# The first two chunk pairs of a Mamba-2 scan in chunks of 64 tokens instead of 128

## The chip, the cores and the metric

The kernel runs on one core of one Trainium2 chip. The metric is the device time of one execution in microseconds. The core has a matrix engine (TensorE, "PE" in the profile, with its weight loads as "PEld"), a vector engine ("DVE"), a scalar engine ("ACT"), a general engine ("POOL") and a queue engine that issues transfers ("SP"). Each executes its own instructions in the order in which the program lists them, and waits for the others by semaphores.

## What is computed

The reference is a Mamba-2 scan followed by a feed-forward block with a parametric ReLU, all in float32:

```python
# x (4, 8, 768, 32), a (4, 8, 768), B and C (4, 8, 768, 16); chunks of 32 tokens
la = log(clip(a, 1e-6, 1)); cum = cumsum(la within the chunk)
L  = exp(cum[i] - cum[j]) for i >= j, else 0
y  = ((C B^T) * L) @ x  +  (C @ state) * exp(cum)
state = exp(sum(la)) * state + sum_j exp(cum[-1] - cum[j]) * B[j] (outer) x[j]
# bridge: (batch, head, token, d) -> (batch * token, head * d) = (3072, 256)
h = X @ w_in                                  # w_in (256, 2048)
g = max(h, 0) + alpha * min(h, 0)
out = g @ w_out                               # w_out (2048, 256)
```

The size of the chunk is free: any size gives the same result, since the state carries over what lies before the chunk.

## The kernel before

**The scan.** The kernel works in chunks of `Q = 128` tokens, two at a time: a pair `gp` holds 256 tokens of one batch entry, and there are 12 pairs. For each pair it needs, per chunk and head, a matrix of decays between two tokens, the gram matrix C B^T, their product `dec` (times the input x gives the part within the chunk), the gain of the state `dps`, the state `new`, a copy of the state masked into head blocks (`sm`), and C decayed (`cd`, times `sm` gives the part from before the chunk). The results, turned into features by tokens, are copied into `xT`, which holds four chunks (a group of `GT = 512` tokens). Pairs 0 and 1, which fill the first group, are written out by hand in `first_two` (line 792); pairs 2 to 11 go through the generator `pair` (line 552) in stages that are woven into the feed-forward work. Pairs from 6 on (`half`) are already computed with each chunk in two halves of 64 tokens, in another way.

**The decays** come from a scan along the tokens on DVE: `dec[t] = a[t] * dec[t-1] + identity[t]`, started afresh by a zero in `a`. For pairs 0 and 1 the row of `a` of each head is spread to all partitions by matmuls with a column of the identity (`spread_rows`, line 490, for pair 0; `spread`, line 504, for pair 1), into PSUM; each of the eight scans then covers 512 columns (lines 908 and 855). Pairs from 2 on get the spread rows by a transfer from a scratch in DRAM (`z`) into the tile `abc`. The running product of decays from a chunk's start (`pf`, tile `ap`) and to its end (`pr`, turned into `prt`, which scales B into `bn` in `pair_loads`, line 465) are computed on 96 rows at a time: `rows_clamp`, `rows_scan`, `rows_out` (lines 411 to 441), and `rows_turn` (443) transposes `pr`, and with it the slopes `alpha`.

**The order of `first_two`.** There is no planner: the order of the text is the order on each engine's queue. Pair 0: spread, scans, transposes of B and C (`turned`, line 804: four PE transposes, one ACT copy `bc`, two ACT multiplies `cz`), gram, state gain (`added`, 827), products of gram and decays (`times`, 849; two of pair 0's four and one of pair 1's run on POOL, after an ACT copy of the gram into SBUF), then `outputs` (859), which multiplies by the masked state and by x and copies into `xT`. For pair 1 the order is: spread, transposes, then the first two hidden tiles of pair 0's tokens (`hidden_two`, line 1003), state gain, gram, the next two hidden tiles, outputs. Then the text outside goes on with hidden tiles of pair 1's tokens, with a pass of `hidden` (991) for every further tile of the group, one `output` (1028) a tile, four tiles behind, and pairs 2 to 4 in between.

`hidden_two` issues eight matmul instructions of 256 columns, two ACT multiplies by `s_alpha`, and returns the two DVE instructions (line 1023) that make the parametric ReLU:

```python
        for i in range(2):
            if t0 == 0:
                gts[g, f + i] = gp.tile([P, GT], F32, name="gt")
            nc.scalar.mul(gts[g, f + i][:, ts], hp[:, i * nt : (i + 1) * nt],
                          s_alpha[:, f + i : f + i + 1])
```

**The weights** arrive in 16 pieces as 64-bit numbers (`raw`) and are converted on the chip: `convert_a` (two or three ACT instructions, line 265 on, and one POOL instruction, 267), `sign` (DVE, 286), `convert_b` (DVE, 296), and `convert` (POOL, 318). `pieces[0]` and `pieces[1]` are the parts of `w_in` that the first four hidden tiles need. Piece 0 must be converted before the first `hidden_two`.

**Buffers.** PSUM has eight banks: two of the pool `ps_s` (`ss`), two of `ps_h` (`hp`, handed out by `spare`), and four single ones (`bank(0)` to `bank(3)`). The pool `gp` has 16 buffers for the hidden tiles `gt`. In the start all transfers but one (`rows`, by ACT) are issued by SP, in the order of the text: pair 0's loads, two weight pieces, `z` and `pf` to DRAM (`rows_out`), pair 1's loads, `pf` back for pair 1 (`load_second`), weight pieces, pair 2's loads.

After the first group, PE does the feed-forward block by a fast matrix product (`quad` and `product`, lines 1121 and 1089), which the change doesn't touch.

Of the kernel before, what the change touches and what calls it, by code (L numbers as in the profile page):

```python
# [9 lines left out]
F32 = mybir.dt.float32  # L10
# [12 lines left out]
def kernel(  # L23
# [196 lines left out]
    def load_second():  # L220

        rows = scratch["pf", 0].rearrange("(b h c) t -> b h (c t)", b=2, h=H)
        nc.sync.dma_start(out=loads["p", 1][3], in_=rows[0, :, 2 * Q : 4 * Q].unsqueeze(1)
                          .to_broadcast([H, N, 2 * Q]))
# [98 lines left out]
    def keep_warm(to, n, cols=2 * Q):  # L323

        for i in range(n):
# [6 lines left out]
    ident_h = const.tile([P, H * Q], F32, name="ident_h")  # L332
    nc.vector.tensor_copy(out=ident_h.rearrange("p (h t) -> p h t", h=H),
                          in_=ident.unsqueeze(1).to_broadcast([P, H, Q]))
# [17 lines left out]
    nc.vector.memset(ends[:, Q - 1 :], 1.0)  # L352

# [35 lines left out]
    def identity_bank():  # L389


        m5_bank.append(bank(3))
        nc.scalar.copy(out=m5_bank[0][:, HT:], in_=ident_h[:, :HT])
        ident_p.append(m5_bank[0][:, HT:])
# [15 lines left out]

    def rows_clamp(i):
        rows = loads.pop(("r", i))
        d0 = prep.tile([RW, SQ], F32, name="r0")
        nc.vector.tensor_scalar(out=d0[:, :Q], in0=rows, scalar1=1e-6, scalar2=1.0,
                                op0=ALU.max, op1=ALU.min)
        if i:
            nc.vector.tensor_scalar(out=d0[:, Q + 1 :], in0=rows[:, HQ + 1 :], scalar1=1e-6,
                                    scalar2=1.0, op0=ALU.max, op1=ALU.min)
        held[i] = d0
# [22 lines left out]

    def rows_turn(i, pr):

        ps = ss_tile() if i else ps_s.tile([P, 512], F32, name="ss")
        nc.tensor.transpose(ps[:, :RW], pr, ident[:RW, :RW])
        if i == 0:
            nc.tensor.transpose(ps[:, RW : RW + NF], al_n, ident[:NF, :NF])
        else:
            nc.tensor.transpose(ps[:, RW : 2 * RW], held["prs"], ident[:RW, :RW])  # L450
        t = bat.tile([P, RW], F32, name="prt")
        if i == 0:
            nc.scalar.copy(out=t, in_=ps[:, :RW])
        for v in range(2 if i else 0):
# [6 lines left out]
        if i == 0:  # L461
# [3 lines left out]
    def pair_loads(gp):  # L465
# [8 lines left out]
        else:  # L474
            pj = prt[i].rearrange("p (b h c) -> p b c h", b=2, h=H)[:, bi, c : c + 2]
# [6 lines left out]
    def first_a(ap, eng):  # L482

        z = prep.tile([P, 2, Q], F32, name="z", bufs=2)
        eng.memset(z[:, :, :1], 0.0)
        eng.tensor_scalar(out=z[:, :, 1:], in0=ap.rearrange("p (k t) -> p k t", k=2)[:, :, 1:],
                          scalar1=1e-6, scalar2=1.0, op0=ALU.max, op1=ALU.min)
        return z

    def spread_rows(z):  # L490

        ts = [bank(r) for r in range(4)]
        for k in range(2):
            for e in range(2):
                for r in range(4):
                    rs = slice(32 * r, 32 * r + 32)
                    row = 32 * r + N * e
                    cs = slice((2 * k + e) * Q, (2 * k + e + 1) * Q)
                    nc.tensor.matmul(ts[r][:, cs], ident[rs, row : row + 1].to_broadcast([32, P]),
                                     z[rs, k], start=(k == 0 and e == 0), stop=True,  # L500
                                     tile_position=(32 * r, 0), skip_group_check=True)
        return ts

    def spread(z, k, tile=lambda w: ss_tile()):

        ts = [tile(w) for w in range(2)]
        for q in range(4):
            for w in range(2):
                rs = slice(64 * w, 64 * w + 64)
                row = 64 * w + N * q  # L510
                nc.tensor.matmul(ts[w][:, q * Q : (q + 1) * Q],
                                 ident[rs, row : row + 1].to_broadcast([64, P]), z[rs, k],
                                 start=(q == 0), stop=True, tile_position=(64 * w, 0),
                                 skip_group_check=True)
        return ts
# [276 lines left out]
    def first_two():  # L792


        nat0, _, xt0, ap0 = loads["p", 0]

        dec = [work.tile([P, 2, H, Q], F32, name="dec") for i in range(2)]
        first = dec[0].rearrange("p a b t -> p (a b t)").rearrange(
            "p (r c) -> p r c", r=4)
        by_bank = first.rearrange("p r (k e t) -> p r k e t", k=2, e=2)  # L800
        pf0 = prep.tile([P, Q], F32, name="pf")
        new = {}
# [13 lines left out]

        def gram_of(bc, cz, banks):
            gram = [t.rearrange("p (k h t) -> p k h t", k=2, h=2) for t in banks]
            for k in range(2):
                for r in range(4):  # L820
                    rs = slice(32 * r, 32 * r + 32)
                    nc.tensor.matmul(gram[r][:, k].rearrange("p h t -> p (h t)"), bc[rs, k],
                                     cz[rs, :, k], start=True, stop=True,
                                     tile_position=(32 * r, 0), skip_group_check=True)
            return gram

        def added(dps, bn, xt):
            for k in range(2):
                for r in range(4):
                    rs = slice(32 * r, 32 * r + 32)  # L830
                    nc.tensor.matmul(dps[rs, k], bn[:, k, rs],
                                     xt[:, k, 2 * r * D : 2 * (r + 1) * D],
                                     start=True, stop=True, tile_position=(0, 32 * r),
                                     skip_group_check=True)

        def mask(sm, new, ks):
            n = ks.stop - ks.start
            nc.gpsimd.tensor_tensor(
                out=sm.rearrange("p k (g m) -> p k g m", g=2),
                in0=new[:, ks].unsqueeze(2).to_broadcast([P, n, 2, 2 * D]),  # L840
# [3 lines left out]
        def copied(gram):  # L844
            g0 = op.tile([P, GT], F32, name="o_sb").rearrange("p (k h t) -> p k h t", k=2, h=2)
            nc.scalar.copy(out=g0, in_=gram)
            return g0

        def times(i, r, gram, eng=nc.vector):
            o = dec[1][:, :, 2 * r : 2 * r + 2] if i else by_bank[:, r]  # L850
            eng.tensor_tensor(out=o, in0=gram, in1=o, op=ALU.mult)

        def decays(k, w, t):
            ws = slice(512 * w, 512 * w + 512)
            nc.vector.tensor_tensor_scan(out=dec[1][:, k].rearrange("p h t -> p (h t)")[:, ws],
                                         data0=t, data1=ident_h[:, ws], initial=0.0,
                                         op0=ALU.mult, op1=ALU.add)

        def outputs(i, tiles, st, cd, xt, ws, warm=0):
            y = [t[:, : 2 * Q].rearrange("p (k t) -> p k t", k=2) for t in tiles]  # L860
            keep_warm(y[ws[0]].rearrange("p k t -> p (k t)"), warm)
            begun = False
            for k in range(2):
                if st[k] is None:
                    continue
                for q in range(4):
                    qs = slice(32 * q, 32 * q + 32)
                    for w in range(KC):
                        hs = slice(64 * w, 64 * w + 64)
                        nc.tensor.matmul(y[w][qs, k], st[k][hs, qs], cd[hs, k],  # L870
# [601 lines left out]
```

## Time and profile before

| what | value |
|---|---|
| median of 3 runs | 358.48 us (358.33 to 358.49) |
| profiled execution, its own time | 358.82 us |
| span of the profiled execution | 357.1 us |
| granted TensorE clock | 1.000 |
| first hidden tiles' matmuls (line 1011) start | 18.02, 21.35, 25.01 us |
| first matmul of line 996 starts | 28.94 us |
| end of the scans of pair 0 (line 908) | 10.99 us |
| end of the last scan of pair 1 (line 855) | 20.07 us |

The span runs from the first to the last instruction of the execution, and times within it count from its start. The profile's page gives the busy time of each engine, the chain of waits (the work that ended last, followed back step by step), and the groups of instructions by line, with their count, busy time and the mean duration of one in ns. "x32 128x64" is 32 instructions on 128 partitions by 64 columns; a float32 matmul call appears as two instructions. A matmul's duration includes its way through the array, so that durations of neighbours overlap; the distance between two starts is what the engine spends on one.

### The profile page before, as it was taken

How to read it: one execution, taken by the hardware profiler on the slowest of the kernel's cores; microseconds unless marked ns; L12 is line 12 of the kernel's file. 1: busy time of each engine (PE TensorE's matmuls, PEld its weight loads, DVE VectorE, ACT ScalarE, POOL GpSimd, SP SyncE). 2: the span in 40 equal slices, each digit the busy share in tenths (PEclk: the TensorE clock that was granted, in tenths of full speed). 3: DMA queues.
4: the chain of work that ended last, by engine and by line, in shares of the span. 5: the costliest groups of instructions: out<-in, count | busy, mean ns of one | idle time of the engine just before them, and what ended most of it. 6: DMA issues, size and time to landing. Idle time of an engine off the chain costs nothing.

```text
span 357.1 us, 7561 instructions
## 1 busy us (share of the span) xinstructions
PE 350.5 (98%) x2894; PEld 289.0 (81%) x2894; DVE 240.0 (67%) x467; ACT 174.0 (49%) x387; POOL 205.0 (57%) x221
## 2 busy tenths in 40 slices
PE   8899999999999999999999999999999999999995
PEld 8676666578888888888888888888888888888884
DVE  6987986998748856857747856757856633653363
ACT  3577666535355346345345445345445344444431
POOL 4876668589938855725646626647527535533520
PEclk9999999999999999999999999999999999999999
DMA  7899999608255403403513423513001002002004
GB/s 112 175 189 299 334 202 255 143 16 168 89 97 125 98 2 75 104 2 75 96 39 74 91 48 68 93 49 64 10 4 29 0 2 31 0 0 32 0 1 91
DMA packets 105470, 30.19 MB, mean 85 GB/s; under 512 B 79881, under 2 KB 101337, under 8 KB 105433
## 3 DMA queue, kind: packets, MB, share of 16 engines
q1 hardware_dynamic: 105048, 29.52, 37.7%
q8 instruction: 23, 0.38, 0.4%
q10 hardware_dynamic: 384, 0.18, 0.2%
q14 instruction: 15, 0.11, 0.1%
HBM read 26.32 MB, written 3.37 MB: 83 GB/s over the span
## 4 chain that ended last, share of the span: by engine, by line
PE 93%; SPq 3%; DMA 1%; ACT 1%; issue 0%; DVE 0%
PE bank L1108 33%; PE hp L1133 29%; PE bank L1034 8%; PE hp L996 6%; PE ss L1133 6%; SPq L188 2%; PE hp L1011 2%; PE ss L758 1%; PE ss L702 1%; DMA nat<-in_C_dram 1%; PE bank L1101 1%; PE ss L750 1%; PE ss L776 1%; PE ss L713 1%; PE ss L589 1%; PE ss L768 0%
## 5 line engine op out<-in xcount | busy, mean ns | idle before, releaser
L1190 POOL TENSOR_TENSOR gt<-gt 128x512 f32<-128x512 f32 x58 | 74.1, 1278 | 21.1 <-DVE gt L1118 16.3
L1108 PE MATMUL bank<-gt,w_out 128*128 128x256 f32 x320 | 83.5, 381 | 0.0
L1108 PEld LDWEIGHTS bank<-gt,w_out 128*128 128x128 f32 x320 | 60.1, 190 | 9.2 <-issue 1.0
L1118 DVE SCALAR_TENSOR_TENSOR gt<-hp,s_mul,gt 128x256 f32<-128x256 f32 x96 | 42.0, 479 | 29.1 <-ACT gt L1116 26.8
L1180 POOL TENSOR_TENSOR gt<-gt 128x512 f32<-128x512 f32 x20 | 25.4, 1268 | 62.6 <-DVE gt L1118 57.2
L1116 ACT ACTIVATE gt<-hp,s_alpha 128x256 f32<-128x256 f32 x96 | 40.3, 471 | 34.6 <-PE hp L1133 31.5
L1108 PE MATMUL bank<-gt,ws 128*128 128x256 f32 x224 | 55.9, 379 | 0.0
L1108 PEld LDWEIGHTS bank<-gt,ws 128*128 128x128 f32 x224 | 42.3, 190 | 5.6
L1133 PE MATMUL hp<-xs,w_in 128*128 128x256 f32 x160 | 41.9, 384 | 0.0
L1133 PE MATMUL hp<-xs,ws 128*128 128x256 f32 x160 | 41.2, 380 | 0.0
L1159 DVE TENSOR_TENSOR hp<-hp,u 128x512 f32<-128x512 f32 x20 | 14.0, 699 | 35.8 <-ACT u L1157 35.8
L1133 PEld LDWEIGHTS hp<-xs,ws 128*128 128x128 f32 x160 | 30.3, 190 | 4.3 <-POOL xs L1075 0.2
L1133 PEld LDWEIGHTS hp<-xs,w_in 128*128 128x128 f32 x160 | 29.7, 190 | 4.5
L1034 PE MATMUL bank<-w_out,gt 128*128 128x256 f32 x128 | 31.0, 384 | 0.0
L1034 PEld LDWEIGHTS bank<-w_out,gt 128*128 128x128 f32 x128 | 23.6, 190 | 6.5 <-issue 2.9
L1133 PE MATMUL ss<-xT,w_in 128*128 128x256 f32 x96 | 24.6, 379 | 0.0
L996 PE MATMUL hp<-xT,w_in 128*128 128x512 f32 x48 | 22.7, 596 | 0.2 <-DVE gt L1023 0.2
L616 POOL TENSOR_TENSOR sm<-state,bmask 128x256 f32<-128x256 f32 (+1 forms) x10 | 6.2, 619 | 28.9 <-DVE state L613 28.9
L532 DVE TENSOR_TENSOR_SCAN dec<-abc,bank 128x192 f32<-128x192 f32 x48 | 22.7, 522 | 0.0
L1148 ACT COPY m<-hp 128x512 f32<-128x512 f32 x8 | 4.7, 586 | 35.7 <-PE hp L1133 35.7
L1157 ACT COPY u<-hp 128x512 f32<-128x512 f32 x20 | 11.7, 585 | 19.4 <-PE hp L1133 19.4
L1118 DVE SCALAR_TENSOR_TENSOR gt<-c,s_mul,gt 128x256 f32<-128x256 f32 x40 | 20.6, 555 | 0.0
(204 smaller groups left out, 618.3 us busy)
## 6 DMA issues: line engine op xcount, KB each, us to landing
abc<-z SPq DMA_DIRECT2D x24, 192.0 KB
raw<-in_moe_w_in_dram SPq DMA_DIRECT2D x8, 512.0 KB
raw<-in_moe_w_out_dram SPq DMA_DIRECT2D x8, 512.0 KB
abc<-z SPq DMA_DIRECT2D x8, 512.0 KB
out_dram<-o_sb SPq DMA_DIRECT2D x32, 64.0 KB
nat<-in_B_dram SPq DMA_DIRECT2D x26, 64.0 KB
nat<-in_C_dram SPq DMA_DIRECT2D x24, 64.0 KB
xt<-in_x_dram SPq DMA_DIRECT2D x12, 128.0 KB
```

Of the source, the lines that this page charges most:

```text
L188: nc.sync.dma_start(out=nat[:, i, k].rearrange("p (h n) -> p h n", h=H), in_=src[b, :, ts, :].rearrange("h p n -> p h n"))
L532: nc.vector.tensor_tensor_scan(out=dv[:, o : o + SQ], data0=abc[k][:, s : s + SQ], data1=ident_p[0][:, :SQ], initial=0.0, op0=ALU.mult, op ...
L996: nc.tensor.matmul(hp, w_in[:, k, f * P : (f + 1) * P], xts[g][:, k], start=(k == 0), stop=(k == KC - 1))
L1034: nc.tensor.matmul(pos[0][t // 2][:, t % 2], gt[:, t * Q : (t + 1) * Q], w_out[:, f], start=(f == 0 and t % 2 == 0), stop=(f == NF - 1), s ...
L1108: nc.tensor.matmul(ms[g][i][:, h], w, blocks[g, z][n][:, p], start=(q == 0 and h == 0), stop=(q == NQ - 1), skip_group_check=True)
L1116: nc.scalar.mul(o[:, p], h[:, p], s_alpha[:, fs[p]])
L1118: nc.vector.scalar_tensor_tensor(out=o[:, p], in0=h[:, p], scalar=s_mul[:, fs[p]], in1=o[:, p], op0=ALU.mult, op1=ALU.max)
L1133: nc.tensor.matmul(to[:, p], w(2 * z + p), b, start=start and p == 0, stop=True, skip_group_check=True)
L1157: nc.scalar.copy(out=u2, in_=A)
L1159: nc.vector.tensor_tensor(out=Y, in0=Y, in1=u2, op=ALU.add)
L1180: nc.gpsimd.tensor_tensor(out=tc_, in0=g22, in1=g12, op=ALU.subtract)
L1190: eng.tensor_tensor(out=o, in0=x0, in1=x1, op=ALU.subtract)
```

## The change

Pairs 0 and 1 are computed in chunks of 64 tokens. A pair then has four chunks `c`, of which two lie on the lower half of the partitions and two on the upper half (`k, j = divmod(c, 2)`: `k` is the old chunk of 128, `j` the half of it). A matrix of decays is 64 by 64 instead of 128 by 128: a scan covers 256 columns instead of 512, and so does a product with the gram, whose four products per pair all run on DVE from PSUM. Spread, gram, state gain and products with x are issued for each half by itself, with 64 instead of 128 rows or columns of the array. There are four states a pair instead of two, with as many masked copies. B, C and x are loaded as before and lie as before in SBUF.

Since pairs from 2 on keep chunks of 128, the rows of decays are made twice: once for chunks of 64 (`rows_short`, for pairs 0 and 1, written to a DRAM scratch `short`), and once as before (`rows_clamp`, now on POOL for the first half of the rows, `rows_scan`, `rows_out`), later in the order. Constants and small tiles for this are put into four buffers of `gp` (`lent`) and one of `xsp`. The order of `first_two` is changed with it; in pair 1 the transposes now come after the first hidden tiles.

The core of the diff:

```diff
     def load_second():
-        rows = scratch["pf", 0].rearrange("(b h c) t -> b h (c t)", b=2, h=H)
+        rows = scratch["short", 0].rearrange("(b h c) t -> b h (c t)", b=2, h=H)
...
-    ident_h = const.tile([P, H * Q], F32, name="ident_h")
-    nc.vector.tensor_copy(out=ident_h..., in_=ident.unsqueeze(1).to_broadcast([P, H, Q]))
+    ident_q = const.tile([P, 4 * HQ], F32, name="ident_q")
+    for v in range(2):
+        vs = slice(HQ * v, HQ * (v + 1))
+        nc.vector.tensor_copy(out=ident_q[vs].rearrange("p (c t) -> p c t", c=4),
+                              in_=ident[vs, vs].unsqueeze(1).to_broadcast([HQ, 4, HQ]))
...
+    lent = [gp.tile([P, 4, Q], F32, name="gt", tag="gt") for i in range(4)]
+    ends_q = lent[3][:, 0]
+    nc.vector.memset(ends_q, 0.0)
+    nc.vector.memset(ends_q[:, HQ - 1 :: HQ], 1.0)
+    starts_r = lent[3][:, 1]
+    nc.gpsimd.memset(starts_r, 0.0)
+    starts_a = lent[0][:, :2].rearrange("p k t -> p (k t)")
+    nc.gpsimd.memset(starts_a, 0.0)
...
+    def rows_short(r, rows):
+        clamp(nc.vector, starts_r[:RW, ::HQ], rows[:, ::HQ])
+        nc.vector.memset(r[:, ::HQ], 0.0)
+        pr = lent[3][:RW, 2]
+        nc.vector.tensor_tensor_scan(out=pr[:, ::-1], data0=r[:, 1:][:, ::-1],
+                                     data1=ends_q[:RW, ::-1], initial=0.0, ...)
+        rpf = lent[3][:RW, 3]
+        nc.vector.tensor_tensor_scan(out=rpf, data0=r[:, :Q], data1=starts_r[:RW], ...)
+        scratch["short", 0] = dr.tile([RW, Q], F32, name="short0")
+        held["short"] = rpf
+        return pr
...
+        def spread(z):
+            ts = [bank(r) for r in range(4)]
+            for e in range(2):
+                for r in range(4):
+                    rs = slice(32 * r, 32 * r + 32)
+                    row = 32 * r + N * e
+                    for j, hs in enumerate(halves):
+                        o = ts[r][hs, : 2 * Q].rearrange("p (k e t) -> p k e t", k=2, e=2)
+                        nc.tensor.matmul(o[:, :, e], ident[rs, row : row + 1]
+                                         .to_broadcast([32, HQ]), z[rs, :, hs], start=e == 0,
+                                         stop=True, tile_position=(32 * r, HQ * j), ...)
+            return ts
+        def scan(i, r, t):
+            nc.vector.tensor_tensor_scan(out=dec[i][:, r], data0=t[:, : 2 * Q], data1=ident_q, ...)
         def gram_of(bc, cz, banks):
...
-                    nc.tensor.matmul(gram[r][:, k].rearrange("p h t -> p (h t)"), bc[rs, k],
-                                     cz[rs, :, k], start=True, stop=True,
-                                     tile_position=(32 * r, 0), skip_group_check=True)
+                    for j, hs in enumerate(halves):
+                        o = banks[r][hs, (2 + k) * Q : (3 + k) * Q]
+                        nc.tensor.matmul(o.rearrange("p (e t) -> p e t", e=2), bc[rs, k, hs],
+                                         cz[rs, :, k, hs], start=True, stop=True,
+                                         tile_position=(32 * r, HQ * j), skip_group_check=True)
+        def x_products(y, xt, i):
+            for w in range(KC):
                 for k in range(2):
                     for q in range(4):
                         h = 4 * w + q
+                        for j, hs in enumerate(halves):
+                            d = dec[i][hs, h // 2].rearrange("p (k e t) -> p k e t", k=2, e=2)
+                            nc.tensor.matmul(y[w][j][32 * q : 32 * q + 32, k],
+                                             xt[hs, k, h * D : (h + 1) * D], d[:, k, h % 2],
+                                             tile_position=(HQ * j, 32 * q), ...)
+        def state_products(y, i, cd):
+            for c in range(4):
+                k, j = divmod(c, 2)
+                if i or c:
+                    s = sm[i][:, c - 1] if c else sm[0][:, 3]
+                    for w, ws in enumerate(halves):
+                        nc.tensor.matmul(y[w][j][:, k], s[ws], cd[ws, k, halves[j]], ...,
+                                         tile_position=(HQ * w, 0), skip_group_check=True)
+        def copy_out(i, y):
+            for w in range(KC):
+                o = xts[0][:, w, 2 * i * Q : 2 * (i + 1) * Q].rearrange(
+                    "p (k j t) -> p j k t", k=2, j=2)
+                for j in range(2):
+                    nc.scalar.copy(out=o[:, j], in_=y[w][j])
...
+        z0 = first_a(ap0, nc.vector, lent[1][:, :2])
+        sp = spread(z0)
+        prq = rows_short(rq, rows)
+        clamp(nc.vector, starts_a[:, ::HQ], ap0[:, ::HQ])
+        nc.sync.dma_start(out=scratch["short", 0], in_=held.pop("short"))
+        load_pair(1)
+        load_second()
+        rows_clamp(0)
+        for r in range(4):
+            scan(0, r, sp[r])
+        nc.vector.tensor_tensor_scan(out=pf0, data0=z0..., data1=starts_a, ...)
+        rows_turn("short", prq)
+        tp = spare()
+        bc0, cz0 = turned(nat0, tp)
+        bn0 = pair_loads(0)
+        cd0 = decayed_c(bc0, pf0)
+        z1 = first_a(loads["a", 1], nc.gpsimd, lent[1][:, 2:])
         pr = rows_scan(0)
         rows_out(0)
-        load_pair(1)
-        load_second()
         load_next(2)
         load_pair(2, False)
...
         hp = spare()
         keep_warm(hp, 6, Q)
+        gram_of(bc0, cz0, sp)
+        dps = dps_in([hp, tp])
+        added(dps, bn0, xt0)
+        for r in (0, 1):
+            times(0, r, sp[r])
+        states(0, dps, pf0)
+        for r in (2, 3):
+            times(0, r, sp[r])
+        mask(0, slice(0, 3))
+        slopes(alpha)
         convert_a(*pieces[0])
+        y = places([hp, tp], [ss(), ss()])
+        sp = spread(z1)
         xts[0] = xtp.tile([P, KC, GT], F32, name="xT")
+        x_products(y, xt0, 0)
+        state_products(y, 0, cd0)
+        copy_out(0, y)
+        sign(*pieces[0])
+        for r in (0, 1):
+            scan(1, r, sp[r])
+        convert_b(*pieces[0])
+        for r in (2, 3):
+            scan(1, r, sp[r])
+        convert_next()
         convert_a(*pieces[1])
+        rows_turn(0, pr)
+        bn1 = pair_loads(1)
         sign(*pieces[1])
         convert_next(first=False)
+        prelus = [hidden_two(0, 0, 0, spare())]
+        own = [ss(), ss()]
+        bc1, cz1 = turned(nat1, own[1])
+        cd1 = decayed_c(bc1, pf1)
+        mask(0, slice(3, 4))
+        dps = dps_in(own)
+        added(dps, bn1, xt1)
+        states(1, dps, pf1)
+        gram_of(bc1, cz1, sp)
+        mask(1, slice(0, 4))
+        for r in range(4):
+            times(1, r, sp[r])
         slope_signs()
         convert_a(*pieces[2])
         prelus.append(hidden_two(0, 2, 0, spare()))
         prelus[0]()
         convert_next(first=False)
         prelus[1]()
+        y = places(own, [bank(0), bank(1)])
+        x_products(y, xt1, 1)
+        state_products(y, 1, cd1)
+        copy_out(1, y)
...
     load_next(2)
-    rows_clamp(0)
     FIRST = 4
     first_two()
```

## The prediction

> **What bounds the kernel now.** I read the page's busy shares first, then its chain of waits, then busy time by stage, then the timeline of the first 30 us. The first windows below are the start, the last three all that follows (columns after the width: busy us of PE, PE's weight loads, DVE, ACT, POOL, then clock and DMA share).
>
> ```profile
> PE 350.5 (98%) x2894; PEld 289.0 (81%) x2894; DVE 240.0 (67%) x467; ACT 174.0 (49%) x387; POOL 205.0 (57%) x221
> ...
> PE 93%; SPq 3%; DMA 1%; ACT 1%; issue 0%; DVE 0%
> ```
>
> ```profile
> 9.00:18.00 9.00, 7.50 (x120) 5.40 (x121) 8.90 (x11) 5.15 (x12) 8.14 (x11) 1.00 0.86 175
> ...
> 24.95:28.90 3.95, 3.72 (x16) 2.87 (x16) 3.38 (x7) 2.96 (x8) 1.95 (x2) 1.00 1.15 174
> 28.90:60.00 31.10, 31.06 (x202) 19.77 (x203) 25.10 (x42) 21.32 (x42) 21.50 (x23) 1.00 1.04 292
> ```
>
> The reader is to see two regimes. From 28.9 us on PE has 0.04 us of idle in 31.1, and none from 60 to 350; a matmul's busy time overlaps its neighbour's, but the chain agrees (each L996 group starts when the L1034 group before it has issued). So what moves the first matmul of L996, at 28.94, moves the end by as much. Before 25 us PE waits, and from 9 to 18 us DVE is busy 8.90 of 9. The change lies wholly in that start. These lines set its pace:
>
> ```profile
> 14.35 2.33 DVE L855 TENSOR_TENSOR_SCAN dec<-bank,ident_h 128x512 f32<-128x512 f32 x2
> 16.34 1.26 POOL L318 TENSOR_TENSOR w_in<-wr,wg 128x512 uint32<-128x512 uint32 x1
> 17.29 0.58 ACT L810 COPY bc<-hp 128x512 f32<-128x512 f32 x1 [0.61 <-PE hp L807]
> 17.90 0.91 ACT L813 ACTIVATE cz<-bc,par 128x256 f32<-128x256 f32 x2
> 18.02 1.97 PE L1011 MATMUL hp<-xT,w_in 128*128 128x256 f32 x8 [0.77 <-ACT bc L810]
> 20.08 0.84 ACT L1017 ACTIVATE gt<-hp,s_alpha 128x256 f32<-128x256 f32 x2 [1.27 <-PE hp L1011]
> 21.35 1.99 PE L1011 MATMUL hp<-xT,w_in 128*128 128x256 f32 x8
> 25.01 3.72 PE L1011 MATMUL hp<-xT,w_in 128*128 128x256 f32 x16
> 28.94 1.96 PE L996 MATMUL hp<-xT,w_in 128*128 128x512 f32 x4 [0.21 <-DVE gt L1023]
> ```
>
> The four L1011 groups are the milestones: 18.02 (after the w_in piece at 17.60 and pair 1's transposed B and C, late by DMA, at 17.87), 21.35, 25.01, and L996 at 28.94. Pair 1's gram products start at 20.27, with no wait: cz was ready at 18.81.
>
> **What the Trainium skill says.** "TensorEngine Tiling (Array Packing)", Key Properties: changing the tiling mode drains the array. The trace agrees: 16 gram issues of 53 ns are 0.85 us, but the next group starts 1.08 us later. "TensorE: Matmul & The Clock Gate", "Wait — 56ns, not 53.3ns?": matmuls never start closer than about 25 ns. The trace disagrees for column tiles: L758 issues 64 of 64 rows by 32 columns in 0.85 us, 13 ns each. I take the trace; the page prices a rival. "SBUF — State Buffer", "SBUF: two separate sides": DVE and POOL share a port pair held for a whole instruction. The trace agrees: L286, beside POOL's L318, took 1.30 us at 16.59, and 0.42 at 12.27.
>
> **Prices.** Scan of 256 columns: L538, four in 2.41 us, 0.60; of 512: 1.20. DVE product of 256: 0.42 (L1211). ACT copy of 128x128: 0.28, between 0.22 (64 columns) and 0.37 (256). POOL on 384 columns: 1.0, between 0.73 and 1.28. PE issue, from L499, L702 and L758: 53, 26 and 13 ns for 128, 64 and 32 output columns, two instructions per call, and 0.27 us to the last one's end.
>
> **Part 1, to the first hidden matmul: earlier by 1.6.** The first spread starts behind the warm matmuls, 4.6 either way. 32 x 26 ns + 0.27 end at 5.7, not 6.39. Four scans of 0.60 run to 8.15, pf0 (256 columns now) to 8.75, rows_scan and rows_out, moved here (0.42 + 0.40 + memsets), to 9.65. Gram cannot profit: it waits for nat0's four loads, transposes 0.57, bc 0.58, cz 0.91. The transposes started at 6.72 with no DMA wait shown, so the loads landed between about 6.0 (two microseconds from the last issue's start at 3.85 are my estimate, from rows: issued 0.79, used by 3.36) and 6.72; I take 6.6, gram at 8.95, bank 0 complete at 9.75. DVE: two products to 10.64; added(0), the ACT copy of state 0 to 10.82; three states of 0.28 to 11.7; two products to 12.55, where before it was 12.35 for all that. The new spread reuses all four banks, so it stalls at its fourth until 12.55; bank 0 is complete at 13.05. sign hides in that. Two scans to 14.25, L296 0.69 to 14.95, POOL's L318 1.26 to 16.25, first L1011 at **16.4** instead of 18.02. POOL is in time: mask to 12.5, the slopes moved behind it (0.69), L267 to 13.8. xT is ready at 16.0: 64 products 1.0 from 13.15, 12 state products of 128 columns 0.75, four copies.
>
> **Part 2, to pair 1's gram: 0.6 later.** The hidden group now stands ahead of pair 1's transposes on PE, and on ACT its two multiplies (0.84) stand ahead of bc and cz. ACT takes them only when the eight matmuls have ended (20.08 after 19.99 in the trace). So: hidden to 18.4; transposes issued at 18.3, done by 18.95; multiplies to 19.3; bc to 19.88; added(1), in the same bank as bc's source, 19.9 to 20.5; cz to 20.8; gram at **20.85** against 20.27. PE is idle for about 1.3 us of this, with gram1 and the second hidden group queued behind, and DVE's four products behind gram1. The 1.6 gained is gone: 0.55 by the transposes that no longer lie in a wait, the rest by ACT's 0.84 and the 1.49 of bc and cz, formerly beside the hidden group.
>
> **Part 3, to the third L1011 group: 1.25 later.** Gram 1.05 to 21.9, hidden 1.92 to 23.82. DVE's states and four products end at 23.45, beside it. Then 64 products 1.0 (before 32 at K=128 with the copy of the first half beside the second), 16 state products 0.95 (before 0.60 for 32), now last: 25.77. The bank of y00 is complete at 25.62, of y01 at 25.83, two copies follow: **26.25** against 25.01. The added 0.65 over part 2 is PE 0.2 and copies that nothing covers.
>
> **Part 4, to L996: 1.15 later.** PE would be there at 26.25 + 3.72 = 29.97. On ACT: the last two copies to 26.77, convert_a 0.68 + 1.14 to 28.6, multiplies to 29.44, second L1023 to 29.95, the handover of 0.15: **30.1** against 28.94. The wait that cost 0.21 is still there.
>
> **Costed at nothing.** ident_q for ident_h (DVE, 0.77 of copy less two small ones) and new memsets: behind the warm matmuls to 4.58; uncovered, 0.3. POOL's two memsets and rows_clamp (about 1 us): POOL idles 3.3 us to 7.14. The gram copies and POOL products that go (ACT 1.8, POOL 4.3) free engines that wait elsewhere; what is late next is the scans' conversion, counted. Lent tiles take 4 of 16 gt buffers: the sixteenth hidden tile comes tens of us later. SP: short (48 KB, one issue of 0.4) takes the place of z and pf ahead of pair 1's loads, so nat1 comes 0.4 us sooner, needed 1.4 later; z and pf move behind load_second, and pair 2's ap<-pf, queued directly behind two weight loads, may now make SP wait for pf to land, up to 2 us, with pair 2's B, C, x and weight loads behind it. The cover: SP was blocked anyway in the x load issued at 19.79 (4.40 us for what takes 0.6). Without it, pair 2's scans (36.75, loads issued 27.3) have some 3 us to spare. Unseen; bounds -0.2 to +0.5, taken 0.
>
> **Sum.** +1.15 on the profiled execution's 358.82 (span 357.1, 1.7 around it) is 359.97; its own time lies 0.34 above the median shown, so 358.48 + 1.15 = **359.6**.
>
> **Rivals.** (a) *Not slower*: ACT's wait in part 2 does not appear. If cz is ready when added(1) has issued, at 19.5 instead of 20.8, gram starts 1.35 sooner and the sum is -0.2: 358.3, and a DVE that keeps its floor in part 1 (0.5 sooner if nat0 lands at 6.0, gram no longer the gate) makes it 357.8. For it: ACT is the least busy engine, 49%. Against: the program order on ACT and the end-of-bank wait at 20.08. Deciding point: gram1 before 19.6. (b) *Heavier*: small tiles pay the page's 25 ns. Each 64-product block grows by 0.75, pair 1's wholly on the path, pair 0's by 0.35 beyond the w_in piece: +2.25, 360.7. Against it L758's 13 ns; for it, that L758 mixes 64 and 128 columns, and no group of 64 alone is in the trace. (c) The halves don't free DVE (scans on 256 columns as slow as 0.9 in such company): +1.8 in part 1, about 361.4; L538 speaks against, I fold it into (b).
>
> **How the numbers follow.** About 0.2%, 0.72 us, is what a measurement of this kernel can tell from no change. My steps 0.52 (358.9 to 360.4; 0.06 of it under 0.72), rival (a) 0.28 (0.12 below -0.72), (b) with (c) 0.20. Slower 0.46 + 0.20 = 0.66, same 0.06 + 0.16 = 0.22, faster 0.12. The range 358.0 to 360.9 leaves out about 0.12 below and 0.08 above.
>
> **What would show it.** Right: first L1011 group near 16.4, gram1 waiting for ACT's cz at about 20.8, third group near 26.2 after two short copies, DVE idle before states(1), PE dense after 30. Wrong: gram1 before 19.6, or L758-like issues at 25 ns, or any new wait on PE after 30 us, which I hold impossible from the profile except pair 2's late loads.

## The result and the profile after

| | before | after |
|---|---|---|
| median (lowest to highest) of 4 runs | 358.40 us (358.22 to 358.49) | 360.93 us (360.74 to 361.46) |
| profiled execution, its own time | 358.82 us | 360.92 us |
| its span | 357.1 us | 359.2 us |
| its granted TensorE clock | 1.000 | 0.986 |

The change makes the kernel slower: the ratio is 1.0067, with a 95% interval of 1.0054 to 1.008. That is +2.53 us, where +1.15 was forecast; 360.93 lies 0.03 above the upper end of the range. The two profiled executions differ by 2.10 only, because what follows the start of PE's last group takes about 0.4 us longer in before's (4.5 us to the end of the span, against 4.0). The last group on PE starts at 352.63 before and at 355.16 after, and this difference is again 2.53.

One condition is needed to read the numbers below: executions of one kernel differ in the granted clock of their first 20 us, so runs whose mean clock is 0.998 or more are called *full clock*, the others *dropped*, and medians are given for each.

The page of the kernel after: busy times, the TensorE clock in 40 slices of 9 us, and the chain's shares by engine.

```profile
PE 351.0 (98%) x2999; PEld 289.5 (81%) x2999; DVE 238.1 (66%) x481; ACT 172.5 (48%) x389; POOL 203.8 (57%) x221
...
PEclk9679999999999999999999999999999999999999
...
PE 93%; ACT 1%; issue 1%; POOL 1%; DVE 1%; SPq 1%; DMA 1%; POOLq 0%
```

The busy shares and the chain hardly moved. The second line is what is new: slices two and three, 9 to 27 us, have 6 and 7 tenths of the clock where before had all of it. In steps of a quarter of a microsecond the clock falls to one half at 11.52 and is back at 21.76 us. The busy time by stage (width; busy us of PE, weight loads, DVE, ACT, POOL with instruction counts; clock; DMA share; GB/s) is therefore shown in stretches of 3.41 us that end at 11.52, a third of the 10.24 between the two; why, comes with the experiments. Kernel after:

```profile
4.69:8.11 3.42, 3.18 (x50) 2.40 (x48) 3.23 (x7) 1.49 (x5) 1.01 (x2) 1.00 1.11 163
8.11:11.52 3.41, 1.69 (x73) 1.02 (x72) 3.17 (x12) 1.70 (x4) 2.43 (x4) 1.00 0.96 302
11.52:14.93 3.41, 3.19 (x92) 2.58 (x94) 2.98 (x7) 0.04 (x1) 2.13 (x6) 0.50 0.82 97
14.93:18.35 3.42, 3.07 (x17) 2.53 (x16) 1.85 (x4) 2.12 (x7) 2.13 (x3) 0.50 0.72 144
18.35:21.76 3.41, 3.12 (x11) 2.08 (x9) 0.31 (x1) 1.38 (x3) 2.02 (x2) 0.50 0.94 295
21.76:25.17 3.41, 2.88 (x70) 2.18 (x70) 2.61 (x9) 2.03 (x4) 2.47 (x4) 1.00 1.02 150
```

PE is busy for 1.69 of the 3.41 us ahead of the drop; it is idle from the end of the state gain at 9.63 to 11.74 but for eight spread matmuls (kernel after; L862 is the state gain, L833 the spread of pair 1, which waits first for POOL and then for DVE's products):

```profile
9.10 0.53 PE L862 MATMUL hp<-xt,bn 64*32 64x64 f32 x32
10.61 0.45 PE L833 MATMUL bank<-gt,ident 32*64 32x128 f32 x8 [0.99 <-POOL gt L425]
11.74 1.45 PE L833 MATMUL bank<-gt,ident 32*64 32x128 f32 x24 [0.68 <-DVE dec L854]
```

At half clock a busy microsecond does about half the work: eight hidden matmuls take 3.67 us instead of 1.97 (below). The kernel before, in the stretch ahead of the drop and during it:

```profile
8.11:11.52 3.41, 2.70 (x47) 2.00 (x47) 3.41 (x5) 2.10 (x5) 2.70 (x7) 1.00 1.00 313
11.52:21.76 10.24, 9.25 (x127) 6.72 (x125) 9.29 (x14) 5.89 (x12) 9.22 (x11) 1.00 0.88 176
```

In this stretch PE also ran two matmuls of ones in the kernel before, which the change leaves out:

```profile
13.30 1.14 PE L326 MATMUL ss<-const-float32-1.0 128*128 128x256 f32 x4
```

DVE is indeed freed by the change: 5.14 us in those 10.24, formerly 9.29, and 6.71 in the run e9 below, where the clock stays at 1.00. From 31.42 on PE is as dense as it was: 28.54 us of the 28.58 to 60 are busy.

The timeline of the kernel after (start, duration, engine, line, operation, count; in brackets the idle time before it and what ended it), in the lines that answer to the milestones of before; L1043 is the old L1011, L1028 the old L996, L849 pair 1's gram:

```profile
14.84 1.27 POOL L318 TENSOR_TENSOR w_in<-wr,wg 128x512 uint32<-128x512 uint32 x1 [1.03 <-DVE wr L296]
16.60 3.67 PE L1043 MATMUL hp<-xT,w_in 128*128 128x256 f32 x8
20.06 1.06 PE L815 MATMUL ss<-ident,nat 128*128 128x128 f32 x4
20.37 0.84 ACT L1049 ACTIVATE gt<-hp,s_alpha 128x256 f32<-128x256 f32 x2 [2.45 <-POOL w_in L318]
21.16 0.59 ACT L818 COPY bc<-ss 128x512 f32<-128x512 f32 x1
21.78 0.91 ACT L821 ACTIVATE cz<-bc,par 128x256 f32<-128x256 f32 x2
22.74 0.70 PE L849 MATMUL bank<-cz,bc 32*64 32x128 f32 x32 [0.49 <-ACT cz L821]
23.37 1.99 PE L1043 MATMUL hp<-xT,w_in 128*128 128x256 f32 x8
27.54 3.72 PE L1043 MATMUL hp<-xT,w_in 128*128 128x256 f32 x16 [0.35 <-ACT xT L917]
31.46 1.96 PE L1028 MATMUL hp<-xT,w_in 128*128 128x512 f32 x4 [0.21 <-DVE gt L1055]
```

The first hidden group starts 1.42 us sooner than before, but its eight matmuls take 3.67 us instead of 1.97, and the transposes behind it take 1.06 (0.60 at full clock, in e9 below). Pair 1's gram waits for ACT's cz, as forecast, and the third hidden group and L1028 start 2.5 us later than before.

### The profile page after: what moved, and what is told of

Read it like the earlier page. It is cut to its first block, busy times and chain, and to the rows that moved or that the text cites. A ratio compares the mean times of both kernels' runs of the same rounds, so it can differ in the third digit from the quotient of the medians.

```text
span 359.2 us, 7798 instructions
## 1 busy us (share of the span) xinstructions
PE 351.0 (98%) x2999; PEld 289.5 (81%) x2999; DVE 238.1 (66%) x481; ACT 172.5 (48%) x389; POOL 203.8 (57%) x221
## 3 DMA queue, kind: packets, MB, share of 16 engines
HBM read 26.32 MB, written 3.42 MB: 83 GB/s over the span
## 4 chain that ended last, share of the span: by engine, by line
PE 93%; ACT 1%; issue 1%; POOL 1%; DVE 1%; SPq 1%; DMA 1%; POOLq 0%
PE bank L1140 33%; PE hp L1165 28%; PE bank L1066 8%; PE hp L1028 6%; PE ss L1165 6%; PE ss L762 1%; PE ss L706 1%; PE hp L1043 1%; PE bank L1133 1%; PE ss L754 1%; PE ss L780 1%; PE ss L717 1%; DMA nat<-in_C_dram 1%; POOL w_in L318 1%; PE ss L593 1%
## 5 line engine op out<-in xcount | busy, mean ns | idle before, releaser
L1028 PE MATMUL hp<-xT,w_in 128*128 128x512 f32 x48 | 22.7, 596 | 0.2 <-DVE gt L1055 0.2
```

The costliest lines, as they stand in the source:

```text
L1028: nc.tensor.matmul(hp, w_in[:, k, f * P : (f + 1) * P], xts[g][:, k], start=(k == 0), stop=(k == KC - 1))
```

## The experiments

Four theories stood against each other. **Clock**: the change leaves PE idle after pair 0's state gain, and it leaves out the `2` in `outputs(…, (1, 0), 2)`, two matmuls of ones whose result nothing uses, which ran at 13.30 before; the clock falls. **Small tiles**: the issues of 64 by 32 themselves cost more or pull the clock down. **Order**: pair 1's gram waits for ACT, because hidden tiles stand ahead of the transposes; moving these gains what the chunks of 64 were to give. **Weights** ("theory 4" where an expectation counts them): time that is won in the start is lost again at 36 to 49 us, where the weight pieces arrive.

Medians in us, with the number of runs; e1 to e4, e5 to e8, and e9 to e11 each ran on one chip, with the kernel before.

| run | overall | ratio to before [95%] | full clock | dropped | before, full clock |
|---|---|---|---|---|---|
| e1_warm | 359.78 | 1.0027 [1.0012, 1.0043] | 359.23 (12) | 361.05 (10) | 358.91 (39) |
| e2_order | 359.75 | 1.0024 [1.0012, 1.0036] | none | 359.75 (6) | 358.91 |
| e3_warm_order | 359.33 | 1.001 [1.0, 1.002] | 359.02 (9) | 359.58 (5) | 358.91 |
| e4_before_cold | 359.30 | 1.0017 [1.0002, 1.0032] | 358.74 (2) | 359.37 (9) | 358.91 |
| e5_after_again | 361.35 | 1.0059 [1.004, 1.0079] | none | 361.36 (8) | 359.00 (55) |
| e6_full_warm | 359.65 | 1.0023 [1.0007, 1.0039] | 359.58 (17) | 361.70 (5) | 359.00 |
| e7_full_warm_split | 359.79 | 1.0029 [1.0012, 1.0046] | 359.53 (15) | 361.61 (7) | 359.00 |
| e8_best | 358.89 | 0.999 [0.9975, 1.0005] | 358.83 (18) | 360.21 (3) | 359.00 |
| e9_full_warm3 | 359.10 | 1.0019 [1.0004, 1.0035] | 359.08 (20) | 361.88 (2) | 358.82 (36) |
| e10_order_split2 | 358.93 | 0.9994 [0.9982, 1.0005] | 358.82 (12) | 359.30 (2) | 358.82 |
| e11_order_split2_raw4 | 358.53 | 0.9999 [0.9978, 1.0019] | 358.31 (10) | 360.93 (4) | 358.82 |

### Keeping PE busy: e1, e5, e6, e9

e1 adds eight matmuls of ones (128 columns) in the idle stretch:

```diff
         added(dps, bn0, xt0)
+        others = [ss(), ss()]
+        keep_warm(others[0], 8, Q)
```

> The changed kernel with eight idle matmuls of 128 columns after pair 0's state gain, where PE waits from 9.5 to 11.7 us. Theory 1 (the clock): the changed kernel left out the two warm matmuls that stood before pair 0's outputs, PE idles most of 9.5 to 11.7, and the granted clock falls to 0.5 until about 20.6; with PE kept busy the clock stays at 1.0, the first hidden group starts near 16.2 and takes 1.95 instead of 3.67, pair 1's gram starts near 20.8 instead of 22.74, line 1028's first matmul near 30.0 instead of 31.46, and the time is 359.3 to 359.8. Rival (small tiles): matmuls on quarter arrays don't count as activity, so the clock falls all the same and the time stays within 0.3 of the changed kernel's 360.9. Rival (order alone): the clock falls but costs nothing, since ACT's order decides pair 1's gram; clock 1.0, time unchanged.

The changed kernel as it is dropped its clock in all twelve runs (four of the result, eight of e5); with the eight matmuls 12 of 22 runs keep it, at 359.23. The profile of e1 was one of the dropped ones (kernel e1, by stage):

```profile
9.72:13.14 3.42, 3.42 (x89) 2.93 (x78) 3.13 (x11) 1.47 (x3) 2.68 (x6) 1.00 1.06 264
13.14:16.55 3.41, 2.28 (x78) 1.72 (x79) 3.41 (x6) 1.14 (x5) 2.17 (x4) 1.00 0.88 113
16.55:19.96 3.41, 3.41 (x9) 2.55 (x10) 0.78 (x2) 0.94 (x3) 2.97 (x3) 0.50 0.65 156
19.96:23.38 3.42, 2.14 (x70) 1.48 (x69) 1.08 (x5) 3.17 (x7) 1.14 (x2) 1.00 1.05 289
```

The first hole is filled (3.42 of 3.42), the clock stays at 1.00 through it and through the small tiles behind it, and it falls at 16.55, after the next hole. It is back 3.41 us later; the first hidden group lies in that stretch and again takes 3.67 us.

e5 is the changed kernel again, unaltered.

> The changed kernel once more, on the chip of the next three, since the runs there scatter more than the first ones. Theory 1 (the clock falls after PE's idle from 9.5 to 11.7): the time is again some 2.5 above before, 360.5 to 361.2, with a clock of 0.5 for some 9 us. Rival (the clock's phase against the program decides each time): the time scatters over 2 us or more from run to run.

It gave 361.35, so the result holds on another chip. e6 fills the two later holes as well:

```diff
         for r in (0, 1):
             scan(1, r, sp[r])
+        keep_warm(sp[0][:, 2 * Q :], 6, Q)
...
         bc1, cz1 = turned(nat1, own[1])
+        keep_warm(sp[1][:, 2 * Q :], 4, Q)
```

> The changed kernel with idle matmuls in all three of PE's waits (8 after pair 0's state gain, 6 after its outputs, 4 behind pair 1's transposes, of 128 columns). Theory 1: the clock is 1.0 throughout, the first hidden group starts near 16.4 and takes 1.95, gram of pair 1 near 20.8, line 1028 near 30.0, which is the timetable of the prediction; time 359.2 to 359.8, 1.2 to 1.7 below the changed kernel on the same chip. Rival (ACT's order alone makes the loss): time within 0.4 of the changed kernel's.

17 of 22 runs keep the clock. But six are too many: they start at 16.04 and push the first hidden group to 17.56, 1.52 us behind their own start. e9 has three in their place, and 0.86 us from their start to the hidden group.

> As the kernel with idle matmuls in all three waits, but only three instead of six behind pair 0's outputs, where six ran past the arrival of the first weight piece and held the first hidden group back by a microsecond. Theory 1: at full clock the group starts at 16.4 to 16.7, pair 1's gram near 20.8 to 21.1, the third group near 25.6, line 1028's first matmul near 29.5 to 29.8, so that the changed kernel at full clock is 0.3 to 0.8 above before; runs in which the clock falls are some 1.8 longer. Rival: at full clock it is still over 1 above before, as the prediction's sum of 1.15 said.

20 of 22 runs keep the clock, at 359.08. Its profile (clock 0.999) shows the changed kernel's timetable without the drop, with fifteen matmuls of ones in its holes (e9's timeline; L1047 and L1032 are L1043 and L1028, L296 is DVE's part of the conversion of the first weight piece):

```profile
14.13 0.69 DVE L296 SCALAR_TENSOR_TENSOR wr<-wt,wr 128x512 uint32<-128x512 uint32 x1 [0.24 <-POOL wt L267]
16.31 1.98 PE L1047 MATMUL hp<-xT,w_in 128*128 128x256 f32 x8
20.69 0.70 PE L849 MATMUL bank<-cz,bc 32*64 32x128 f32 x32 [0.49 <-ACT cz L821]
25.49 3.72 PE L1047 MATMUL hp<-xT,w_in 128*128 128x256 f32 x16 [0.35 <-ACT xT L917]
29.41 1.96 PE L1032 MATMUL hp<-xT,w_in 128*128 128x512 f32 x4 [0.20 <-DVE gt L1059]
```

So the measured 2.52 at the last line (31.46 against 28.94) is 0.47 of timetable (29.41 against 28.94) and 2.05 of clock (31.46 against 29.41). This split compares single profiles. The medians agree on the second part: full clock against dropped within one kernel is 1.82 in e1, 2.12 in e6, 2.08 in e7 and, with only two dropped runs, 2.79 in e9. On the first, full clock against before at full clock gives +0.26 (e9), +0.32 (e1) and +0.58 (e6).

### Are small tiles to blame? e4

e4 takes the idle matmuls after the start out of the kernel *before*, most of whose tiles there have 128 rows or columns:

```diff
         hp = spare()
-        keep_warm(hp, 6, Q)
...
-        outputs(0, (ss(), ss()), (None, sm0[0][:, 0]), cd0, xt0, (1, 0), 2)
+        outputs(0, (ss(), ss()), (None, sm0[0][:, 0]), cd0, xt0, (1, 0))
```

> The kernel before without its idle matmuls after the start (six of 128 columns before pair 0's gram, two of 256 before its outputs). Theory 1: the clock falls here too, in chunks of 128, some 3 to 4 us after PE's waits at 8 to 11 us, and the time grows by 1 to 2.5, to 359.5 to 361. Rival (small tiles): without quarter arrays the clock stays at 1.0 and the time at 358.4 or a little below.

The clock drops in 9 of 11 runs, and the time goes up by 0.46 among those (359.37 against 358.91), less than the 1 to 2.5 expected. Its profile by stage:

```profile
5.50:8.91 3.41, 1.85 (x30) 1.18 (x22) 2.84 (x4) 1.66 (x5) 1.28 (x3) 1.00 1.05 171
8.91:12.33 3.42, 3.22 (x38) 2.25 (x40) 2.87 (x4) 1.21 (x4) 2.05 (x6) 0.50 1.08 317
12.33:15.74 3.41, 3.41 (x46) 3.10 (x44) 3.03 (x5) 2.47 (x5) 3.25 (x4) 0.50 0.60 55
15.74:19.15 3.41, 2.64 (x56) 1.98 (x41) 3.32 (x4) 2.24 (x5) 2.88 (x4) 1.00 1.02 186
```

An idle PE lowers the clock with large tiles too, and e9 runs all the small tiles at 1.00. Small tiles are neither needed for the drop nor enough for it. The drop costs a quarter of what it costs in the changed kernel: it is over at 15.74, and the first hidden group starts at 18.36 instead of 18.02. What a drop costs depends on what runs in it, and not on its length alone: e1's, half as long but with the first hidden group inside, costs 1.82.

**The length of a drop.** It is 10.24 us in the result's profile, 3.41 in e1's, and 6.83 in those of e2 (13.40 to 20.23), e4 (8.91 to 15.74) and e5 (12.73 to 19.56): three, one and two times 3.41. This fits a clock that is decided anew every 3.41 us, by a window whose phase differs from run to run. In the windows just ahead of the five drops PE is busy for 1.69, 2.28, 1.88, 1.85 and 1.67 us. The window of 3.41 us, wherever it is laid, that holds least of PE's work in the start has 2.42 in before's profile, 2.50 in e9's, and 1.88 in e3's (13.0 to 16.4); all three kept the clock. It may be that an unlucky phase finds such a hole and another one doesn't, so that a kernel drops in part of its runs. That is not shown: nothing here set the phase, and e7, whose profile (at full clock) has no window under 2.92, still dropped in 7 of 22 runs.

### The order: e2, e3, e8

```diff
-        prelus = [hidden_two(0, 0, 0, spare())]
         own = [ss(), ss()]
-        bc1, cz1 = turned(nat1, own[1])
+        bc1, cz1 = turned(nat1, own[0])
+        prelus = [hidden_two(0, 0, 0, spare())]
```

> The changed kernel with pair 1's transposes moved ahead of the first hidden group again (into the other of the two banks), so that ACT takes bc and cz before the hidden group's multiplies. The clock still falls. Theory 2 (ACT's order): of the loss, the wait of pair 1's gram on cz (PE idle about 1.3 us at 21.3 to 22.7) goes; gram starts near 21.2 to 21.6 instead of 22.74, time 359.4 to 360.0. Rival (the clock is all): the transposes at half clock ahead of the hidden group delay it by as much as is won, time within 0.3 of 360.9.

> Both edits: idle matmuls in PE's wait and pair 1's transposes ahead of the hidden group. Theories 1 and 2 together: hidden group near 16.3 to 16.9, pair 1's gram right behind added(1) at about 19.5, the second hidden group near 20.6 (its weight piece is ready at 20.4), line 1028 near 28.8 to 29.0 and the time 358.1 to 358.6, no slower than before. If only one of the two costs something, the time is that of the better single edit.

With the order alone the clock drops in all six runs, and still the time is only 0.84 above before's on its chip, where the changed kernel has 2.53 (2.36 in e5): gram comes at 21.18 with no wait for ACT, and L1028 at 29.89. With e1's matmuls added (e3) gram comes at 19.59 and the first matmul of line 1030, which answers to L996, at 28.53, 0.41 ahead of before. Yet the full-clock median is 359.02 against 358.91, where 358.1 to 358.6 was expected. e3's timeline shows where the lead goes (PEld is the weight load of a matmul, L1068 the output pass, old L1034):

```profile
19.59 0.69 PE L849 MATMUL bank<-cz,bc 32*64 32x128 f32 x32
28.53 1.95 PE L1030 MATMUL hp<-xT,w_in 128*128 128x512 f32 x4 [0.21 <-DVE gt L1057]
31.35 0.69 ACT L265 ACTIVATE wt<-raw 128x512 f32<-128x512 f32 x1 [2.15 <-DMA raw<-in_moe_w_in_dram]
...
38.24 1.59 PEld L1068 LDWEIGHTS bank<-w_out,gt 128*128 128x128 f32 x8 [0.81 <-POOL w_out L318]
...
47.22 1.59 PEld L1068 LDWEIGHTS bank<-w_out,gt 128*128 128x128 f32 x8 [1.26 <-POOL w_out L318]
```

ACT waits for a weight piece, conversions on POOL follow late, and PE's weight loads wait for them, at 38 and at 47 us. Before's group at 48.40 comes at 49.06: a lead of 0.41 has become a lag of 0.66. That is more than a fixed arrival of the weights would explain. Before converts the piece that ACT waits for here at 30.59, without a wait; in e3 SP waits 2.25 us for `pf` to land in DRAM before it issues pair 2's `ap<-pf` (17.82 to 20.07), which the new order of transfers brings, and issues that piece of weights at 26.43 instead of 26.16. e8 adds e6's eight and six matmuls and the split of e7 (below) to the new order.

> All edits: idle matmuls in two of the waits, pair 1's transposes ahead of the hidden group, the split copies. By the timetable alone line 1028 starts near 27.9 to 28.3 and the time is 357.5 to 358.0. Theory 4 (the weights): from 28 to 48 us the conversion of the weights, which arrive at full transfer load, allows no start of line 1028 before about 28.9, and what is gained above that is lost in PE's waits on POOL's conversion near 40 to 48; time 358.0 to 358.6, no different from before.

It is level with before (358.83 against 359.00 at full clock; the ratio's interval includes 1), though the first matmul that answers to L996 is 0.3 sooner, at 28.64 (27.9 to 28.3 was expected). Its ACT waits for weight pieces are 1.7 at 31 us and 1.5 at 38.

### The copies that nothing covers: e7

e7 is e6 with pair 1's state products first, and its x products and copies by halves of the features (the flags that start and end the sums change with it, not shown):

```diff
-        x_products(y, xt1, 1)
         state_products(y, 1, cd1)
-        copy_out(1, y)
+        for w in range(KC):
+            x_products(y, xt1, 1, (w,))
+            copy_out(1, y, (w,))
```

> As the last, and pair 1's products with the states moved ahead of those with x, the copies into xT of the first half of the features beside the second half's products. Theory 3 (part 3 of the prediction: copies that nothing covers): the third hidden group starts 0.5 to 0.7 sooner, line 1028 0.3 to 0.6 sooner, time 358.8 to 359.4. Rival (ACT's conversion of the next piece ahead of the multiplies decides line 1028): the third group comes sooner, line 1028 and the time stay within 0.15.

The third hidden group comes 4.65 us after gram instead of 4.79, a gain of 0.14 where 0.5 to 0.7 was expected, with a wait of 0.17 for ACT instead of 0.35. In the medians it is 359.53 against 359.58, nothing that these runs can tell from zero.

### The cap: e10, e11

e10 is e8 with two instead of six matmuls; e11 also issues one weight piece ahead of pair 2's loads:

```diff
         load_next(2)
+        load_next(1)
         load_pair(2, False)
-        load_next(2)
+        load_next(1)
```

> Idle matmuls (8 and 2), pair 1's transposes ahead of the hidden group, split copies. Hidden group near 16.9, gram 19.2, line 1028 near 28.0. Theory 4 (the weights' arrival caps the gain): ACT waits for the fifth weight piece until about 31 and PE for the conversion of the eighth near 47; the time is within 0.4 of before on this chip. Rival (no cap): 0.7 to 1.0 below before.

> As the last, with the fifth weight piece loaded ahead of pair 2's B, C and x instead of behind them. Theory 4: ACT's wait for it at 31 goes (the piece lands near 28), and the time falls by 0.2 to 0.6 against the kernel without this edit, unless the next piece (the seventh, near 38) then limits in its place, when it stays within 0.2. Rival (pair 2's loads are as tight): pair 2's transposes wait, the time rises by 0.5 or more.

ACT's longest single wait for a piece of w_in falls from 2.7 to 1.5 us, and the weight loads' waits for `w_out` in the output pass go from 2.3 us in total to 0.6 (the lists of waits at 28 to 62 us, first e10's and then e11's):

```profile
ACT wt L265 <- DMA raw<-in_moe_w_in_dram: 2.9, 2, 2.7
...
PEld bank L1071 <- POOL w_out L318: 2.3, 2, 1.3
```

```profile
ACT wt L265 <- DMA raw<-in_moe_w_in_dram: 1.5, 1, 1.5
...
PEld bank L1072 <- POOL w_out L318: 0.6, 1, 0.6
```

e11's group that answers to before's at 61.49 starts at 60.77, so the lead of 0.72 lasts. At full clock e11 is at 358.31, 0.51 under before and under e10. This is the best version, but the gain is not established: four of its 14 runs dropped the clock, the ratio over all runs is 0.9999 [0.9978, 1.0019], and the profiles of e10 and e11 are the longest and the shortest of their full-clock runs.

## Why the prediction was right, and where its size was wrong

**The sign** held, but mostly by luck. The timetable on which it rested is worth +0.26 to +0.58 us in the medians at full clock, less than the 0.72 that the prediction itself called no change; what lifts the result clear of that is the clock, which it didn't forecast. The waits that it named are there: the chunks of 64 free DVE, but pair 1's gram then waits for ACT. e9, the changed kernel at full clock, tests the timetable step by step.

| step | predicted | e9 | the term |
|---|---|---|---|
| Part 1, first hidden group | 16.4 | 16.31 | held, by two misses that cancel |
| Part 2, pair 1's gram | 20.85 | 20.69 | held; the wait for cz is there, 0.49 |
| Part 3, gram to third group | 5.40 | 4.80 | sized 0.60 too long |
| Part 4, third group to L996 | 3.85 | 3.92 | held; the wait of 0.20 is there |

**Part 1** ends where it should by another way. DVE is ahead: pair 0's products end at 11.97 (forecast 12.55) and the first two scans of pair 1 at 13.89 (14.25). But POOL's part of the conversion, "in time" in the forecast at 13.8, ends at 14.10, and DVE's L296 waits 0.24 for it.

**Part 3** was mis-sized in two terms. Gram was taken at 1.05, from the old 1.08 for 16 instructions; the new 32 release the next group after 0.63 (20.69 to 21.32). The 64 products with x were taken at 1.0; they take 0.79 (23.24 to 24.03, 12 ns each). The 16 state products took 0.96, forecast 0.95, and the wait for copies is there.

**What failed is the assumption under every price: that the clock stays at 1.00.** The prediction had the facts. Its part 1 lets gram end at about 9.75 and the new spread stall until 12.55, which is an idle PE for most of that time, and the diff takes the warm argument out of `outputs`. It booked neither: an idle engine that nothing waits for was costed at nothing, and the two matmuls of ones were not on the list of what the change removes. The drop that this left out is 2.05 of the 2.52 us at L1028. The idle time is what the profiles tie it to: the clock falls at 11.52 in the result's profile and at 12.73 in e5's, while the spread, behind which the two matmuls of ones stood, ends at 13.19 and 13.39. They would have come too late to prevent it; whether they would have shortened it was not tried. The Trainium skill, "TensorE: Matmul & The Clock Gate", "What's actually happening", says that PE falls to half rate after an idle window of about 3.4 us, and that the window runs freely, so that the place of the change varies. The traces agree on the half (0.50), on the window (drops of 3.41, 6.83 and 10.24 us) and on the varying place (11.52 us in the result's profile, 12.73 in e5's). They add that the window needn't be idle throughout: with PE busy in half of it, the clock fell; in the result's profile no wait of PE in the window ahead of the fall is longer than 0.99 us.

**The end.** "PE dense after 30" held: the shift is 2.52 at 31.46 and 2.53 at the last group. Two errors partly cancelled: with its own part 3 and the clock's 2.05 the sum would have been about +3.2.

**Costed at nothing**, and rightly for this kernel: SP's new waits. `ap<-pf` for pair 2 is issued at 18.65, 0.33 after the weight load ahead of it has been issued (17.85 and 0.47 long). The wait of "up to 2 us" is real all the same: it is 2.25 us in e3.

**Rival (a)** named its deciding point, gram before 19.6. The changed kernel's is at 20.69 even at full clock, so it fell. What it hoped for comes where the order is changed: e3's gram is at 19.59. But its estimate of what that brings was too high, since an earlier start is not passed on 1:1. The prediction read the dense PE as "what moves the first matmul of L996 moves the end by as much". For a delay this held; a gain was lost at the arrival of the weights, and of e3's lead nothing was left at 49 us.

**Rival (b)** came nearest in time, 360.7, with the wrong cause: 12 ns per product instead of its 25. The number would have been no evidence for it. **Rival (c)** fell with the scans: four of 256 columns take 2.43 us, 0.61 each.

**Open**: what exactly the window counts. PE's busy time alone doesn't decide: 2.28 us led to a drop in e1, and 2.14 in the window from 19.96 did not. Nor was it tried whether tiles of 64 by 32 count for less: in the result's profile the window of 92 matmuls, 64 of them such tiles, was busy for 3.19 us and did not bring the clock back, and one of 11 large ones with 3.12 did. But the window between them, with no such tile and 3.07 us busy, did not either, nor did e4's first at half clock (3.22 us, none of its tiles 64 by 32). No experiment set the window's phase.

## What to carry to other kernels

Idle time of PE ahead of the critical path is not free: read the granted clock by stage beside PE's busy time, and when a change opens a hole that leaves PE busy for only half to two thirds of some 3.4 us, or takes out matmuls that keep PE busy without a result, price half speed for what runs in the next one to three times 3.4 us, as a case of its own. A dense PE passed a delay on 1:1 here, but lost a gain at the next arrival from memory (e3, e10; e11, which loads one piece earlier, kept it in its profile, without a gain that the runs establish). Look for the wait that is just hidden there before booking an earlier start as time won. When an engine is relieved by a reordering, check which engine the reordered work now queues on.

## What the runs showed of the hardware that was not expected

- A drop lasts whole windows of 3.41 us (one, two, two, two and three in five profiles), and one follows a window with PE busy for 1.67 to 2.28 us. The kernel before itself had a mean clock under 0.998 in 17 of 147 runs on these three chips, in nine of them 0.995 or less, which is what one whole window costs.
- Eight matmuls of ones held it in 12 of 22 runs, fifteen in three places in 20 of 22, eighteen in the same three places in 17 and 15 of 22 (e6, e7). They cost nothing that shows in e9's milestones (its first hidden group starts at 16.31, the changed kernel's at 16.60), and 0.66 us of the timetable where they were too many: from the start of e6's six to the hidden group it is 1.52 us (1.53 in e7), from e9's three 0.86. The rest of the 1.25 us between the hidden groups of e6 and e9 is a later start of the six.
- Tiles of 64 rows by 32 columns issue every 12 ns. Gram's 32 instructions on half the columns let the next group start after 0.63 us; its 16 on all columns did so after 1.08.
